# Attention and two feed-forward layers in one program: the second batch's values by probabilities in plain float32, and a new table of ranks

## The chip, the core and the metric

The kernel runs on one core of one Trainium2 chip. Five engines work side by side, each through its own list of instructions, strictly in order: TensorE (PE in the rows; its weight loads are PEld), VectorE (DVE), ScalarE (ACT), GpSimd (POOL) and SyncE (SP), which issues nearly all DMAs. They wait for each other by semaphores. The metric is the device time of one execution in microseconds (us). Three runs of the kernel before gave 1352.32, 1354.08 and 1358.2 us, a median of 1354.08.

## The reference

```python
# attention: batch 4, heads 8, seq 1152, head_dim 64
q_pool = q.reshape(B, H, S // 2, 2, D).mean(axis=3)          # 576 queries a head
scores = scale * np.matmul(q_pool, k.transpose(0, 1, 3, 2))
scores = scores - np.max(scores, axis=-1, keepdims=True)
attn = np.exp(scores)
attn = attn / (np.sum(attn, axis=-1, keepdims=True) + 1e-09)
x = np.matmul(attn, v)                                       # to 2304 tokens x 512
# first layer, d_ff 2048
r = np.maximum(x @ w_in, 0.0)
x = (s * (r * r) + b) @ w_out
# second layer, d_ff 1536
gate = 1.0 / (1.0 + np.exp(-(x @ w_gate)))
out = (gate * (x @ w_val)) @ w_out2
```

The weights come as 64-bit floats and are decoded on the chip.

## The kernel before

Nearly every product is done in three matmuls of the reduced type float32r: an operand is split into a high part (a rounding copy) and a low part (the remainder, a subtraction), and high by high, high by low and low by high add up in one bank of PSUM. The splits are work of ACT, POOL and DVE; the matmuls are work of PE.

Attention goes by batches and, in each, by 4 pairs of heads. The first batch is computed with queries as rows (`pair_rows`). The other three go by half heads (288 queries of one head; 16 to a batch) in `half_head_sums`. For each half head `scores` computes nine chunks of 128 keys by 288 queries (line 1350), copies them to three tiles `st` of 864 columns (ACT, line 909), takes a running maximum (DVE, line 915), turns that on PE (line 1363), reduces it (DVE, line 1367), spreads it over rows on PE (line 1324), subtracts it (DVE, line 915) and takes the exponential (ACT, line 1376). Then come the values by the probabilities. `split_p` makes a high copy (line 902 on ACT or 904 on POOL) and a low remainder (line 912, POOL or DVE) of each `st` tile in `pp` tiles. In batches 2 and 3 (`TWICE`) two matmuls a chunk follow, with the sums of the probabilities taken apart. In batch 1, the second one, three follow: line 1410 has [high values, ones] by the high probabilities, line 1411 the low values by the same, line 1416 [high values, ones] by the low probabilities; the block of ones gives the sums. The stationary tile `vt` (two of them, one to a head of a pair) holds 64 columns of low values, 64 of high values and 64 ones for each of nine chunks. `pair_prep` loads the values to `vn` and splits them into `vt`.

When a batch's attention is done, its tokens go through both layers (`feed`), 512 tokens for each of the first three feeds and 768 for the last. The first feed also decodes all weights: a DMA brings each block to `raw`, POOL, ACT and DVE turn it into float32 and split it, and a second DMA writes it to DRAM, from which the later feeds fetch it. So the attention of batch 1 runs beside the feed of batch 0, that of batch 2 beside the feed of batch 1, and so on.

What stands where in each engine's list is decided while the program is built. Each piece of work is handed to `Plan.add` with the engines that may do it and a key: the place `plan.here` on a scale (set by `ATTENTION` and `FEED`), plus a rank, plus an offset from the table `MOVED` under the work's name, or under the name with the batch's number behind it. `Plan.order` goes through a modelled time, and each free engine takes, of the work that is ready and for which buffers are free (`ROOM`: 6 `st`, 6 `pp`, 2 `vt`), the one with the lowest key. Work that may go to either of two engines goes to the one that is free.

Of the kernel before, what the change touches and what calls it, by code (L numbers as in the profile page):

```python
# [28 lines left out]
    yy=3, h=6, fo=6,  # L29
# [3 lines left out]
TWICE = (2, 3)  # L33
BANKS = {"wd", "pr", "ps", "pm", "acc", "ff", "p2", "sw"}
# [3 lines left out]
ATTENTION = (0.0, 154.358, 482.727, 814.266, 1198.726)  # L38
FEED = ((155.318, 486.674), (486.244, 871.22), (847.424, 1217.864), (1188.829, 2055.108))
# [3 lines left out]
    "q load": -46.791,  # L43
    "q load 0": 44.454,
    "q load 1": 86.533,
    "q load 2": 91.042,
    "k load": 232.645,
    "k load 0": -178.11,
    "k load 1": 67.466,
    "k load 2": -156.159,  # L50
    "v load": 220.491,
    "v load 0": 331.827,
    "v load 1": 667.448,
    "v load 2": 367.841,
    "v hi": 1.473,
    "v hi 1": -105.009,
    "v hi 2": 255.85,
    "v hi 3": -133.093,
    "v lo": -208.396,
    "v lo 0": -30.837,  # L60
    "v lo 1": -341.63,
    "v lo 3": -230.048,
    "q add": 25.255,
    "q add 0": -41.984,
    "q add 1": 44.956,
    "q add 2": 255.451,
    "q twice": 586.792,
    "q twice 0": 599.338,
    "q twice 2": 363.453,
    "q twice 3": 493.346,  # L70
    "pr qT": 40.098,
    "pr qT 0": -34.388,
    "pr qT 2": -687.648,
    "pr qT 3": -170.944,
    "pr q hi False": 8.875,
    "pr q hi False 1": -50.718,
    "pr q hi False 2": 14.122,
    "pr q hi False 3": 37.589,
    "pr q lo False": -456.003,
    "pr q lo False 1": -96.245,  # L80
    "pr q lo False 2": 251.737,
    "pr q lo False 3": -36.054,
    "pr q hi True": -95.229,
    "pr q hi True 0": 5.606,
    "pr q hi True 1": 326.988,
    "pr q hi True 2": 34.598,
    "pr q lo True": -20.002,
    "pr q lo True 2": -129.941,
    "pr q lo True 3": -59.474,
    "pr kT": 16.556,  # L90
    "pr kT 0": -242.646,
    "pr kT 1": 25.409,
    "pr kT 2": -9.23,
    "pr k hi": -33.36,
    "pr k hi 0": 4.807,
    "pr k hi 1": 196.142,
    "pr k hi 2": -33.136,
    "pr k lo": -142.294,
    "pr k lo 1": -27.449,
    "pr k lo 2": -205.53,  # L100
    "pr k lo 3": 55.312,
    "s b load": 512.259,
    "s b load 1": 1037.217,
    "s b load 2": 943.244,
    "s b load 3": 566.882,
    "r qk 1": -23.623,
    "r qk 1 1": -150.831,
    "r qk 1 2": 82.967,
    "r qk 1 3": -101.691,
    "r max": 331.04,  # L110
    "r max 0": -35.554,
    "r max 1": 131.697,
    "r max 3": 148.081,
    "r - max": -445.953,
    "r - max 0": -517.456,
    "r - max 2": -507.089,
    "r - max 3": -676.096,
    "r exp": 0.445,
    "r exp 1": -55.826,
    "r exp 2": -2.402,  # L120
    "r exp 3": 100.054,
    "r pT": -210.967,
    "r pT 0": -42.303,
    "r pT 1": -113.749,
    "r pT 2": -249.703,
    "r p 1": -48.074,
    "r p 2": -452.662,
    "r p 3": -28.185,
    "r p hi": -16.997,
    "r p hi 0": 14.026,  # L130
    "r p hi 1": -147.871,
    "r p hi 2": 43.781,
    "r p lo": -504.147,
    "r p lo 0": -251.61,
    "r p lo 1": -297.75,
    "r p lo 2": -406.012,
    "r pv": -175.215,
    "r pv 0": -123.32,
    "r pv 1": -108.239,
    "r pv 2": -13.038,  # L140
    "r pT hi 1": 273.656,
    "r pT hi 2": 38.298,
    "r pT hi 3": -483.679,
    "r pT lo": -1383.98,
# [1720 lines left out]
```

## Time and profile before

| | us |
|---|---|
| median of three runs | 1354.08 |
| the profiled execution, whole | 1354.87 |
| its span (first to last instruction) | 1353.0 |
| its mean granted TensorE clock | 0.998 |

A row "a:b" of the table by stretches gives, after the length, how long each engine was busy and its instructions. The span falls roughly into the first batch's attention alone (to 155 us), then the attention of batch 1 beside the first feed (155 to 487), that of batch 2 beside the second feed (487 to 820), that of batch 3 beside the third (820 to 1050), and the last feed. A matmul's busy time overlaps with that of the next, so the distance from start to start tells what one costs in a stream.

### The profile page before, as it was taken

Reading aid. Unit: us, or ns where it says so; the run is one execution under the profiler, and the core shown is the slowest. Engines: PE = TensorE matmul, PEld = TensorE weight load, DVE = VectorE, ACT = ScalarE, POOL = GpSimd, SP = SyncE. Lnnn points to the kernel's source line nnn. Section 1 sums busy time; section 2 is a strip of 40 time slices with the busy share of each in tenths; the row PEclk is TensorE's granted clock in tenths of the full one; section 3 lists DMA queues with packets and bytes.
Section 4 is the critical chain, followed back from the end, with each engine's and each line's share of the span. In section 5 each row is a group of like instructions: output and inputs, shape, how many; then the busy total and the mean of one; then the engine's idle time right before and its main releaser. Section 6 shows DMA issues by size and latency. Waiting matters only on the chain.

```text
span 1353.0 us, 22000 instructions
## 1 busy us (share of the span) xinstructions
PE 1308.0 (97%) x7596; PEld 1167.9 (86%) x7596; DVE 1146.4 (85%) x1857; ACT 925.7 (68%) x1957; POOL 944.1 (70%) x772
## 2 busy tenths in 40 slices
PE   7998999998989999999999999999999999999998
PEld 6887879898877888888888888888888899999997
DVE  6899998999979998999988987998988746678775
ACT  6898889888868777787677758676765354443321
POOL 3578768898978877687757768776766456546562
PEclk9999999999999999999999999999999999999999
DMA  3146325868666682535444444435333434345332
GB/s 97 53 116 215 98 77 183 276 198 281 232 230 229 234 268 102 173 139 173 139 157 154 151 163 160 157 107 205 125 134 124 152 131 154 129 152 185 126 125 47
DMA packets 98279, 214.88 MB, mean 159 GB/s; under 512 B 45148, under 2 KB 67448, under 8 KB 82040
## 3 DMA queue, kind: packets, MB, share of 16 engines
q1 hardware_dynamic: 97000, 213.18, 47.4%
q8 instruction: 60, 0.98, 0.3%
q14 instruction: 51, 0.42, 0.1%
q10 hardware_dynamic: 1168, 0.29, 0.1%
HBM read 173.02 MB, written 40.43 MB: 158 GB/s over the span
## 4 chain that ended last, share of the span: by engine, by line
PE 68%; DVE 9%; ACT 8%; POOL 5%; DMA 5%; issue 5%; SPq 0%; DVEq 0%; POOLq 0%; ACTq 0%
PE banks L985 11%; PE banks L987 11%; PE banks L986 10%; PE banks L1350 5%; PE banks L1698 3%; PE banks L1700 3%; PE banks L1699 3%; PE banks L1122 3%; PE banks L1124 3%; PE banks L1123 3%; PE banks L1416 3%; PE banks L1408 2%; DVE st L915 2%; DMA raw<-in_moe_w_val_dram 2%; PE banks L1506 2%
## 5 line engine op out<-in xcount | busy, mean ns | idle before, releaser
L912 POOL TENSOR_TENSOR pp<-st,pp 128x864 fp32r<-128x864 f32 x94 | 211.3, 2253 | 24.1 <-ACT pp L902 11.9
L915 DVE TENSOR_TENSOR st<-banks,st 128x288 f32<-128x288 f32 x384 | 171.9, 448 | 25.9 <-ACT st L909 10.6
L985 PE MATMUL banks<-xx,w 128*128 128x512 f32 x480 | 193.5, 403 | 0.0
L986 PE MATMUL banks<-xx,w 128*128 128x512 f32 x480 | 188.3, 392 | 0.4 <-POOL xx L912 0.3
L987 PE MATMUL banks<-xx,w 128*128 128x512 f32 x480 | 188.1, 392 | 0.0
L909 ACT COPY st<-banks 128x288 f32<-128x288 f32 x432 | 152.0, 407 | 34.7 <-PE banks L1350 27.2
L1350 PE MATMUL banks<-qT,kT 128*128 128x288 f32 x864 | 159.0, 301 | 5.7 <-ACT st L909 4.1
L915 DVE TENSOR_TENSOR st<-st,banks 128x864 f32<-128x864 f32 x144 | 148.2, 1041 | 3.3 <-PE banks L1324 3.0
L1376 ACT ACTIVATE st<-st 128x864 f32<-128x864 f32 x144 | 133.3, 936 | 24.6 <-DVE st L915 23.6
L1350 PEld LDWEIGHTS banks<-qT,kT 128*128 128x128 f32 x864 | 132.3, 188 | 18.0 <-ACT st L909 4.7
L902 ACT CAST pp<-st 128x864 fp32r<-128x864 f32 x120 | 109.4, 920 | 2.5 <-DVE u L912 1.7
L987 PEld LDWEIGHTS banks<-xx,w 128*128 128x128 f32 x480 | 90.1, 188 | 20.0
L986 PEld LDWEIGHTS banks<-xx,w 128*128 128x128 f32 x480 | 90.4, 188 | 12.6 <-POOL xx L912 1.3
L985 PEld LDWEIGHTS banks<-xx,w 128*128 128x128 f32 x480 | 90.4, 188 | 12.6 <-DVE raw L948 0.4
L986 PE MATMUL banks<-g,w 128*128 128x256 f32 (+1 forms) x256 | 86.6, 338 | 0.6 <-POOL g L912 0.6
L985 PE MATMUL banks<-g,w 128*128 128x512 f32 (+2 forms) x256 | 86.8, 339 | 0.0
L987 PE MATMUL banks<-g,w 128*128 128x512 f32 (+2 forms) x256 | 86.4, 338 | 0.0
L1416 PE MATMUL banks<-pp,vt 128*128 128x288 f32 x432 | 82.1, 299 | 2.5 <-DVE pp L912 1.7
L912 DVE TENSOR_TENSOR pp<-st,pp 128x864 fp32r<-128x864 f32 x50 | 78.1, 1562 | 6.2 <-ACT pp L902 3.7
L912 POOL TENSOR_TENSOR w<-raw,w 128x512 fp32r<-128x512 f32 x58 | 79.4, 1377 | 4.2 <-ACT w L902 3.6
L912 POOL TENSOR_TENSOR pp<-st,st 128x864 f32<-128x864 f32 x21 | 43.3, 2064 | 46.3 <-ACT st L1376 46.3
L1416 PEld LDWEIGHTS banks<-pp,vt 128*128 128x128 f32 x432 | 66.8, 190 | 5.6 <-DVE pp L912 2.4
(248 smaller groups left out, 4004.7 us busy)
## 6 DMA issues: line engine op xcount, KB each, us to landing
w<-d_2g_2v SPq DMA_DIRECT2D x26, 1024.0 KB, 4.9
w<-d_1u_1u SPq DMA_DIRECT2D x24, 1024.0 KB, 4.9
w<-d_1d_1d SPq DMA_DIRECT2D x24, 1024.0 KB, 5.0
w<-d_2d_2d SPq DMA_DIRECT2D x18, 1024.0 KB, 4.8
raw<-in_moe_w_out_dram SPq DMA_DIRECT2D x28, 512.0 KB, 4.3
d_2g_2v<-w SPq DMA_DIRECT2D x12, 1024.0 KB, 7.9
w<-d_2g_2v SPq DMA_DIRECT2D x20, 512.0 KB, 5.3
qn<-in_q_dram SPq DMA_DIRECT2D x16, 576.0 KB, 4.7
```

The costliest lines, as they stand in the source:

```text
L902: nc.scalar.copy(out=out(), in_=in_())
L909: act(name, n, lambda: nc.scalar.copy(out=out(), in_=in_()), r, w, rank, sbuf=False)
L912: shared(name, n, lambda e: ENGINE[e].tensor_tensor(out=out(), in0=in0(), in1=in1(), op=op), r, w, rank, 2.25)
L915: dve(name, n, lambda: nc.vector.tensor_tensor(out=out(), in0=in0(), in1=in1(), op=op), r, w, rank)
L985: nc.tensor.matmul(ps(), lhsT=whi(), rhs=xhi(), start=first, stop=False)
L986: nc.tensor.matmul((ps_lo or ps)(), lhsT=whi(), rhs=xlo(), start=False, stop=False)
L987: nc.tensor.matmul(ps(), lhsT=wlo(), rhs=xhi(), start=False, stop=last)
L1122: nc.tensor.matmul(ps.t[:, :n], lhsT=wt(0, a), rhs=xt(0, a), start=a == 0, stop=False)
L1123: nc.tensor.matmul(ps.t[:, :n], lhsT=wt(0, a), rhs=xt(1, a), start=False, stop=False)
L1350: nc.tensor.matmul(ps.t[:, :HQ], lhsT=kT.t[:, c], rhs=qq[:, w, hf * HQ:(hf + 1) * HQ], start=(w == 0), stop=(w == 1))
L1376: act("exp", 3 * HQ, lambda s=s: nc.scalar.activation(out=s.t[:, :3], in_=s.t[:, :3], func=AF.Exp), [], parts, AT)
L1416: nc.tensor.matmul(acc.t[:, :HQ], lhsT=vt.t[:, 3 * i + c, cols], rhs=lo.t[:, c], start=False, stop=(i == c == 2))
```

## The change

For the heads in `WHOLE`, all eight of batch 1, the values are no longer split: the DMA writes them into the middle third of a `vt` tile of plain float32. The probabilities aren't split either: one plain float32 matmul a chunk takes [values, ones] as the stationary operand and the `st` tile itself as the moving one. `values_slot` gives a `vt` tile of the kind that is wanted; where the kind changes, the block of ones is written anew (four times in the program).

The keys are changed as well: `ATTENTION` and `FEED` have other numbers, and a name now carries the pair of heads (" @0" to " @3") in attention and the quarter of the feed (" :0" to " :3") in a feed, so that `MOVED`, wholly replaced, can give each pair and quarter offsets of its own. So the order on all engines is another one, throughout the program.

```diff
 TWICE = (2, 3)
+WHOLE = [(1, h) for h in range(8)]
...
-ATTENTION = (0.0, 154.358, 482.727, 814.266, 1198.726)
+ATTENTION = (0.0, 153.708, 478.342, 810.481, 1176.021)
...
-    "p hi 1": 23.93,
+    "pv hi @2": 16.166,
...
     def add(self, name, engine, ns, issue, reads=(), writes=(), rank=0, holds=(), port=False):
+        name += self.part
...
+    def values_slot(kind, may):
+        new = []
+        def make(k):
+            if kinds[k] != kind:
+                assert may
+                uid[0] += 1
+                vts[k] = pools["hd"].tile([P, NK, 3 * D], kind, tag=f"vt{k}", bufs=1, name=f"vt{k}_{uid[0]}")
+                kinds[k] = kind
+                new.append(k)
+            return vts[k]
+        t = plan.slot("vt", make)
+        def fill(e):
+            to, of = t.t[:, :, 2 * D:], ones[:, :, None].to_broadcast([P, NK, D])
+            if new and e == "ACT":
+                nc.scalar.copy(out=to, in_=of)
+            elif new:
+                nc.gpsimd.tensor_scalar(out=to, in0=of, scalar1=1.0, scalar2=0.0, op0=ALU.mult, op1=ALU.add)
+        if may:
+            shared("v ones", NK * D, fill, [], [(t, 2)], AT, 0.95, act=0.833)
+        return t
...
+            if whole:
+                dma("v load", P * NK * D * 4, lambda t=t, src=src: nc.sync.dma_start(out=t.t[:, :, D:2 * D], in_=src),
+                    [], [(t, 0), (t, 1)], AT)
+                vt.append(t)
+                continue
...
+            if whole:
+                def issue_whole(s=s, i=i):
+                    for c in range(3):
+                        nc.tensor.matmul(acc.t[:, :HQ], lhsT=vt.t[:, 3 * i + c, D:], rhs=s.t[:, c],
+                                         start=(i == c == 0), stop=(i == c == 2))
+                pe("pv whole", 3 * mm(4 * HQ), issue_whole, [*((s, c) for c in range(3)), (vt, 0), (vt, 2)], [acc], SK)
+                continue
...
+            plan.part = f" :{int(4 * done[0] / total)}"
...
+            plan.part = f" @{hp}"
```

TensorE, the first probabilities of batch 1 by the values, in the kernel before: the three kinds of matmul on a third of a half head.

```order
L1410 MATMUL banks<-pp_2443,vt_111 128x288
L1411 MATMUL banks<-pp_2443,vt_111 64x288
L1410 MATMUL banks<-pp_2443,vt_111 128x288
L1411 MATMUL banks<-pp_2443,vt_111 64x288
L1410 MATMUL banks<-pp_2443,vt_111 128x288
L1411 MATMUL banks<-pp_2443,vt_111 64x288
L1416 MATMUL banks<-pp_2451,vt_111 128x288 x3
```

The same place of the changed program (its line 2559 is the new matmul, 2503 the scores, 2106 to 2108 the first layer, 2516 and 2477 the two steps of the maximum on PE).

```order
L2559 MATMUL banks<-st_2304,vt_1408_2108 128x288 x3
L2106 MATMUL banks<-xx_825,w_998 128x512
L2107 MATMUL banks<-xx_825,w_998 128x512
L2108 MATMUL banks<-xx_825,w_998 128x512
L2503 MATMUL banks<-qT_2142,kT_2211 128x288 x2
L2559 MATMUL banks<-st_2320,vt_1408_2108 128x288 x3
```

Nine float32r matmuls to a third have become three plain ones, which read `st` instead of `pp`.

TensorE, the maximum of batch 1's first half head, before: from the turn of the running maximum (line 1363) to its spreading over rows (line 1324).

```order
L1350 MATMUL banks<-qT_2135,kT_2155 128x288 x6
L1613 MATMUL banks<-ident,r_272_2189 128x128
L1363 MATMUL banks<-ident,st_2238 96x128 x3
L1610 MATMUL banks<-ident,pp_2387 128x128 x4
L1350 MATMUL banks<-qT_2135,kT_2155 128x288 x2
L1324 MATMUL banks<-ident,mc_2417 128x96 x3
```

And in the changed program, from line 2516 to line 2477:

```order
L2503 MATMUL banks<-qT_2143,kT_2212 128x288 x4
L2516 MATMUL banks<-ident,st_2304 96x128 x3
L2503 MATMUL banks<-qT_2143,kT_2212 128x288 x2
L2106 MATMUL banks<-xx_825,w_998 128x512
L2107 MATMUL banks<-xx_825,w_998 128x512
L2108 MATMUL banks<-xx_825,w_998 128x512
L2503 MATMUL banks<-qT_2143,kT_2212 128x288 x2
L2477 MATMUL banks<-ident,mc_2414 128x96 x3
```

Between the two steps PE had four turns and two matmuls of 288 columns; now it has four of 288 and three of 512.

SyncE, the second pair of heads of batch 1, before (`vn` takes the values, `raw` the weights to be decoded):

```order
L1253 DMA kn_3017<-in_k_dram 128x9x64 x2
L932 DMA raw_3059<-in_moe_w_in_dram 128x4x256
L1457 DMA r_d_150<-rs_2910 64x9
L934 DMA raw_3088<-in_moe_w_out_dram 128x1024
L974 DMA d_1d_1d_122<-w_2799 128x2048
L1461 DMA s_2613<-r_d_150 64x288 x2
L974 DMA d_1u_1u_123<-w_2998 128x2048
L1259 DMA vn_3189<-in_v_dram 128x576
L934 DMA raw_3203<-in_moe_w_out_dram 128x1024
```

And in the changed program:

```order
L2395 DMA qn_2857<-in_q_dram 128x1152
L2053 DMA raw_2875<-in_moe_w_in_dram 128x4x256
L2408 DMA vt_1408_2108<-in_v_dram 128x9x64
L2053 DMA raw_2899<-in_moe_w_in_dram 128x4x256
L2400 DMA kn_2917<-in_k_dram 128x9x64 x2
L2095 DMA d_1d_1d_121<-w_2811 128x2048
```

The load of values goes straight to `vt`, with weights and keys queued behind it.

## Rows read from the trace of the kernel before

**Rows 1.** The page's first part: busy time, share, instructions.

```profile
PE 1308.0 (97%) x7596; PEld 1167.9 (86%) x7596; DVE 1146.4 (85%) x1857; ACT 925.7 (68%) x1957; POOL 944.1 (70%) x772
```

**Rows 2.** Stretches: length; busy us (count) of PE, PEld, DVE, ACT, POOL; clock, DMA.

```profile
0.00:155.00 155.00, 134.95 (x914) 120.29 (x915) 134.89 (x302) 131.62 (x384) 102.27 (x132) 1.00 0.41 121
155.00:487.00 332.00, 316.92 (x1975) 281.01 (x1974) 304.16 (x558) 274.29 (x559) 279.01 (x252) 0.99 0.65 212
487.00:820.00 333.00, 329.52 (x1850) 285.35 (x1849) 301.81 (x444) 246.98 (x493) 239.55 (x170) 1.00 0.47 157
```

**Rows 3.** PE in order of time: start us, us, line, operands, count.

```profile
317.18 0.28 PE L985 MATMUL banks<-g,w 128*128 128x256 f32 x1
317.30 0.28 PE L986 MATMUL banks<-g,w 128*128 128x256 f32 x1
...
379.10 0.40 PE L1699 MATMUL banks<-w,g 128*128 128x512 f32 x1
379.33 0.40 PE L1700 MATMUL banks<-w,g 128*128 128x512 f32 x1
...
382.02 0.29 PE L1410 MATMUL banks<-pp,vt 128*128 128x288 f32 x1
...
382.82 0.56 PE L1416 MATMUL banks<-pp,vt 128*128 128x288 f32 x3
```

**Rows 4.** Matmuls of 155 to 487 us by form: count, busy us, mean ns, idle before.

```profile
L985 PE MATMUL banks<-xx,w 128*128 128x512 f32 x160 | 65.2, 407 | 0.0
L1350 PE MATMUL banks<-qT,kT 128*128 128x288 f32 x296 | 57.4, 304 | 5.4 <-ACT st L909 4.1 <-DVE st L915 0.9 <-ACT w L902 0.2
L1410 PE MATMUL banks<-pp,vt 128*128 128x288 f32 x132 | 37.5, 304 | 0.9 <-ACT pp L902 0.9
L986 PE MATMUL banks<-g,w 128*128 128x256 f32 x128 | 36.2, 283 | 0.6 <-POOL g L912 0.6
L1698 PE MATMUL banks<-w,g 128*128 128x512 f32 x32 | 12.8, 400 | 0.0
```

**Rows 5.** PE in order of time, around the one plain float32 matmul, line 1553.

```profile
75.14 0.33 PE L1553 MATMUL banks<-ident,st 128*128 128x64 f32 x2
75.31 0.39 PE L1551 MATMUL banks<-ident,st 128*128 128x128 f32 x2
75.53 0.33 PE L1553 MATMUL banks<-ident,st 128*128 128x64 f32 x2
```

**Rows 6.** A wait of PE in 155 to 487 us: total, times, longest.

```profile
PE banks L1324 <- DVE mc L1367: 4.2, 5, 1.2
```

**Rows 7.** All engines in order of time, around PE's longest wait there.

```profile
385.77 0.65 POOL L937 TENSOR_SCALAR raw<-raw 128x512 f32<-128x512 f32 x1 [4.36 <-DMA raw<-in_moe_w_gate_dram]
386.45 0.73 ACT L940 ACTIVATE raw<-raw 128x512 f32<-128x512 f32 x1 [3.86 <-POOL raw L937]
...
387.51 0.53 PE L1350 MATMUL banks<-qT,kT 128*128 128x288 f32 x2 [4.13 <-ACT st L909]
```

**Rows 8.** Line 1553 alone: records, ns min/median/max, first and last start.

```profile
L1553 PE MATMUL banks<-ident,st x144: 221/248/275, 27.1 to 173.0; 128*128 128x64 f32 x144
```

**Rows 9.** The tile pp in 155 to 487 us, columns as in rows 8.

```profile
L912 POOL TENSOR_TENSOR pp<-st,pp x35: 2045/2074/2865, 189.0 to 479.3; 128x864 fp32r<-128x864 f32 x35
L902 ACT CAST pp<-st x34: 894/922/963, 189.3 to 478.1; 128x864 fp32r<-128x864 f32 x34
...
L904 POOL TENSOR_SCALAR pp<-st x11: 912/920/1714, 188.0 to 452.4; 128x864 fp32r<-128x864 f32 x11
L912 DVE TENSOR_TENSOR pp<-st,pp x10: 1045/1224/2135, 190.4 to 476.0; 128x864 fp32r<-128x864 f32 x10
```

**Rows 10.** DMA issues (count, KB, median us to landing), and a wait of SyncE.

```profile
vn<-in_v_dram SPq DMA_DIRECT2D x32, 288.0 KB, 4.3
kn<-in_k_dram SPq DMA_DIRECT2D x31, 288.0 KB, 4.6
...
SPq L1259 <- POOL vt L912: 70.3, 16, 14.6
```

More of the change, by code (lines that the diff above doesn't have):

```diff
@@ L612, in __init__ @@
         self.room, self.loose, self.banks, self.moved = dict(room), loose, banks, moved
-        self.stage, self.here = 0, 0.0
+        self.stage, self.here, self.part = 0, 0.0, ""
         self.ops, self.last, self.readers, self.queue = [], {}, {}, {}
@@ L1257, in pair_prep @@
             src = v[b, h0 + j].rearrange("(p c) d -> p c d", c=NK)
+            whole = (b, h0 + j) in WHOLE
+            t = values_slot(F32 if whole else F32R, any(divmod(8 * b + h0 + j - i, 8) in WHOLE for i in range(5)))
+            if whole:
[3 more added lines that the diff above has]
+                continue
             vn = slot("ld", "vn", [P, NK, D])
             dma("v load", P * NK * D * 4, lambda vn=vn, src=src: nc.sync.dma_start(out=vn.t, in_=src), [], [vn], AT)
-            t = plan.slot("vt", lambda k: vts[k])
             copy_sb("v hi", NK * D, lambda t=t: t.t[:, :, D:2 * D], lambda vn=vn: vn.t, [vn], [(t, 0)], AT)
@@ L1386, in split_p, with half_head_sums @@
         return hi, lo
-    def half_head_sums(hf, j, qT, kT, vt, x, sums, rows, twice):
+    def half_head_sums(hf, j, qT, kT, vt, x, sums, rows, twice, whole):
         st = scores(hf, qT, kT)
@@ L1416, in issue_lo @@
                     nc.tensor.matmul(acc.t[:, :HQ], lhsT=vt.t[:, 3 * i + c, cols], rhs=lo.t[:, c], start=False, stop=(i == c == 2))
-            pe("pv hi", (3 if twice else 6) * mm(HQ), issue_hi, [hi, (vt, 0), (vt, 1)], [acc], SK)
-            pe("pv lo", 3 * mm(HQ), issue_lo, [lo, (vt, 0), (vt, 1)], [acc], SK)
+            pe("pv hi", (3 if twice else 6) * mm(HQ), issue_hi, [hi, (vt, 0), (vt, 1), (vt, 2)], [acc], SK)
+            pe("pv lo", 3 * mm(HQ), issue_lo, [lo, (vt, 0), (vt, 1), (vt, 2)], [acc], SK)
         if twice:
@@ L1429, in issue_sums @@
                     nc.tensor.matmul(total.t[:D, :HQ], lhsT=vt.t[:, 0, 2 * D:], rhs=u.t[:, w], start=(w == 0), stop=(w == 1))
-            pe("all sums", 2 * mm(HQ), issue_sums, [(u, 0), (u, 1), (vt, 0)], [total], SK)
+            pe("all sums", 2 * mm(HQ), issue_sums, [(u, 0), (u, 1), (vt, 0), (vt, 2)], [total], SK)
             r0 = 0
@@ L1473, in pair_half @@
             at(hf / 2 + j / 4)
-            half_head_sums(hf, j, qT[j], kT[j], vt[j], (xt, xk), sums, D if last else 1, b in TWICE)
+            half_head_sums(hf, j, qT[j], kT[j], vt[j], (xt, xk), sums, D if last else 1, b in TWICE, (b, 2 * hp + j) in WHOLE)
         both = [(sums, 0), (sums, 1)]
@@ L1789 @@
         open_pool(attention, name)
-    vts = [pools["hd"].tile([P, NK, 3 * D], F32R, name=f"vt{k}") for k in range(2)]
+    vts = [pools["hd"].tile([P, NK, 3 * D], F32R, tag=f"vt{k}", bufs=1, name=f"vt{k}") for k in range(2)]
     for t in vts:
         nc.vector.tensor_copy(out=t[:, :, 2 * D:], in_=ones[:, :, None].to_broadcast([P, NK, D]))
+    kinds = [F32R, F32R]
     pairs = [(b, hp) for b in range(B) for hp in range(NP)]
```

1511 lines of the change are left out of this document (980 added, 531 removed), and 670 rows, old and new, of the table MOVED.

## The prediction, made before the changed kernel ran

> **What bounds the kernel now.** I read the busy shares first: PE is busy for 97% of the span, the next engine for 85% [rows 1]. So the question is where PE loses time, and the table by stretches answers it [rows 2]: PE idles for 155.00 - 134.95 = 20 us in the first batch's attention, for 332.00 - 316.92 = 15.1 us beside batch 1, and for only 333.00 - 329.52 = 3.5 us beside batch 2. The two later stretches are alike in PE's work but not in that of the others: ACT has 274 us beside batch 1 and 247 beside batch 2, POOL 279 and 240, DVE 304 and 302, the share of the DMA engines is 0.65 and 0.47.
>
> Busy time hides part of the loss, since a matmul's record overlaps the next. From start to start a matmul of 512 columns costs 379.33 - 379.10 = 0.23 us, one of 256 0.12, and one of 288 0.133: from 382.02 to 382.82 there are six, on lines 1410 and 1411 in turn [rows 3]. Beside batch 1 there are 576 of 512 columns (lines 985, 986 and 987 have 160 each, 1698, 1699 and 1700 have 32 each), 692 of 288 (296 of the scores, 132 on each of lines 1410, 1411 and 1416) and 384 of 256 or 258 (128 on each of lines 985, 986 and 987) [rows 4]; the other 323 of the 1,975 [rows 2] are nearly all transposes, at (75.53 - 75.31) / 2 = 0.11 [rows 5]. That is 132 + 92 + 46 + 36 = 306 us of 332, so some 26 us are lost there, where the idle time says 15. The waits that have a name are on the maximum from DVE, 4.2 us in five pieces [rows 6], and one of 4.1 us on a copy by ACT. That one comes from the stream of weights: POOL had waited 4.36 us for a load of gate weights, ACT's next work for POOL, and PE for ACT [rows 7].
>
> **The change part by part.**
>
> *PE, the price.* Batch 1 has 16 half heads of nine chunks, 144 chunks. Before, each takes three float32r matmuls, 3 x 0.133 = 0.40 us. The trace has no plain float32 matmul of 288 columns, but one of 64, line 1553. One instruction of it stands as two records with a weight load each; the first is followed by the second some 0.055 us later (0.33 for both [rows 5], less the longest record, 0.275 [rows 8]), and from the first start to the next line's it is 75.31 - 75.14 = 0.17 us. 0.055 us for 64 columns is 0.86 ns a column, about two clocks of the 2.4 GHz level (granted 1.00 there [rows 2]); 288 columns at that rate are 0.247 us. Low end: both records run like a float32r one, 0.266 us, or 19 us less than before. High end: the pair scales whole, 0.17 x 4.5 = 0.765 us, 53 us more. I take the value by the first record, two passes of 0.247, 0.494 us: (0.494 - 0.40) x 144 = **+13.5 us**, all on the engine that bounds. The 0.11 us that follow the second record of line 1553 are a weight load that 64 columns don't cover; 288 columns at 0.24 do.
> The Trainium skill, "FP8 and Floating Point Precision", section "TensorE Precision Notes", says that true FP32 takes 4 passes through the array. Reckoned so, 4 x 288 columns at 2.4 GHz are 0.48 us, and the term would be +11.5 instead of +13.5; the trace shows two records, not four, each at about twice the time a column, which is the same amount of work.
>
> *ACT, POOL and DVE, what goes.* Each of the 48 `st` tiles of batch 1 loses a high copy (0.92 us on ACT or POOL) and a low remainder (2.07 on POOL, 1.22 on DVE). In the stretch beside batch 1 these are 34 x 0.92 = 31 us of ACT, 35 x 2.07 + 11 x 0.92 = 83 us of POOL and 10 x 1.22 = 12 us of DVE [rows 9], and the eight splits of the values go too. So there ACT comes to about 240 of 332 us and POOL to about 195, both below what they have beside batch 2; DVE to 290, below its 302 there. None of that is on PE's path by itself: it is worth what PE waited for. What comes in is four writes of ones; nothing of POOL's or ACT's size.
>
> *What PE gets back.* With ACT, POOL and DVE no busier than beside batch 2, PE should lose there in the proportion of batch 2's stretch: 3.5 / 15.1 of 26 us is 6 us. But weights may come late as they did [rows 7], since no weight load goes away, so I leave one such 4.1 us in: about 10 us. That gives back **16 us** of 26; the ends are 0 and 26. The step also drops two links of the chain from exponential to matmul, high copy and remainder, 0.92 + 2.07 us of waiting that PE no longer needs to cover. In return the `st` tile stays held until PE has read it, where the remainder freed it before; six of them are two half heads, so the scores of the next half head but one now wait on PE's own list, not on POOL. That is hidden as long as the first layer's matmuls stand between.
>
> *The loads of the values.* Before, SyncE's load went to a spare `vn` and waited there for POOL, 70.3 us in 16 pieces [rows 10], with POOL's and ACT's splits behind. Now it waits for PE's last read of that `vt`, and weights, keys and queries queue up behind it on SyncE. Each `vt` of a pair has the other head's half between its last use and its next, some 332 / 16 = 20 us against 4.6 us of landing, so I cost it at nothing; uncovered it is a rival below. The load now lands in runs of 64 floats, 256 bytes, as the keys' load already does: 4.6 us against 4.3 [rows 10].
> The Trainium skill, "DMA: Bandwidth & Descriptors", section "Specifications", wants at least 512 bytes for line rate, which speaks against such a load. If that doubled it, each would land some 4 us later; the rows show 0.3, and with 20 us of lead neither changes the sum.
>
> *The new order.* With offsets for each pair and quarter, everything moves. The order shows at batch 1's first maximum that PE has 4 x 0.133 + 3 x 0.23 = 1.2 us of work between turn and spread, where it had 4 x 0.11 + 2 x 0.133 = 0.7: half a us more cover for a step that PE waited for in that stretch [rows 6]. No row prices the rest. PE idles 45 us in all (1353.0 less 1308.0 [rows 1]), 20 of them in the first stretch and 10 after 487 us [rows 2]; those 30 are the low end, -30; the high end is one more stretch that loses like batch 1's, +15. I take **-7**, a quarter of the low end: work on ACT and DVE in the first stretch (132 and 135 of 155 us [rows 2]) is unchanged in kind, so most of its 20 us should stay.
>
> Sum: the profiled execution is 1354.87 us, 0.8 above the median of the runs. 1354.87 + 13.5 - 16 - 7 = 1345.4; I say **1345 us**, 0.7% less.
>
> **Rivals.**
>
> *Only a swap.* PE pays 13.5 us and gets about as much back, because its losses beside batch 1 come less from ACT and POOL than from weights that arrive late and from DVE, which loses only 12 of 304 us. For it: of PE's named waits only 0.9 us is on a copy of the probabilities [rows 4], the longest is the weights' [rows 7], and DVE stays the busiest beside PE. Against it: the loss from start to start is 26 us where the idle time is 15, many small waits rather than a few. Then 1354.87 + 13.5 - 14 = 1354 us.
>
> *The values' load holds up SyncE (slower).* Six of the eight loads stand among the weights to be decoded. Where one stands ahead of its release, the weights behind it come late and PE stops, as before 387.51, for 4.1 us [rows 7]. For it: SyncE has waited up to 14.6 us at such a load [rows 10]. Against it: the 20 us of lead, and that the wait is now for PE alone and no longer for POOL behind it. Price: six times 4.1 is 25 us, and 1354.87 + 13.5 - 16 - 7 + 25 = 1370 us. It decides from three such stops on, for with them the gain is gone.
>
> *The plain matmul costs more than its columns (slower).* If the weight load between the two records isn't covered, the price is 53 us, not 13.5, and the time 1354.87 + 53 - 16 - 7 = 1385 us. Against it: a fixed gap of 0.11 us fits line 1553 better than a factor.
>
> *The new order gives much.* If the first stretch's idle time goes by half and batch 1's loss to 6 us: 1354.87 + 13.5 - 20 - 15 = 1333 us. For it: the table's offsets now differ by pair; against it: that stretch's ACT and DVE are busy for 85 and 87%.
>
> **How the numbers follow.** A measurement of this kernel can tell about 0.5%, 7 us, from no change. Forecast (1337 to 1348): 0.40; the new order gives much: 0.16; only a swap (1348 to 1361): 0.27; the load holds up SyncE: 0.10; the matmul costs more, or the order turns out worse in another stretch: 0.07. 0.5% below the median is 1347.3 and 0.5% above it 1360.9, so the first two make up "faster" but for 0.02, the swap "same", and the rest "slower": faster 0.54, same 0.29, slower 0.17. The range that leaves out a tenth at each end is 1327 to 1364; that of the likeliest alone is the 1337 to 1348 above.
>
> **What would show it right or wrong.** In the profile of the changed kernel line 2559 should stand as 288 records with starts 0.24 to 0.25 us apart; 0.13 or 0.38 would throw the first term out. In the stretch beside batch 1 ACT should be near 240, POOL near 195 and DVE near 290 us, and PE's idle time below 6 us. If POOL and ACT fall like that but PE's waits on DVE and on copies stay, the swap is right. If SyncE waits long at line 2408 and POOL's line for the weights waits for DMA more than before, the third rival is. If batch 1 comes out as said but the total doesn't, look at the first stretch's 20 us.

## The result: slower by half a per cent

| kernel | median, us | runs | ratio to the kernel before, 95% interval |
|---|---|---|---|
| before | 1352.67 | 7 | |
| changed | 1359.98 (1359.04 to 1363.35) | 7 | 1.0052 [1.0036, 1.0068] |

The forecast was 1345 with 0.17 on slower; the time lies inside the wide range, but the likeliest case was wrong, and so was the sign. The changed kernel's profiled execution took 1359.90 us.

The changed kernel's page, its first part, and then its table by stretches, columns as in [rows 1, 2]:

```profile
PE 1317.9 (97%) x7452; PEld 1164.2 (86%) x7452; DVE 1135.7 (84%) x1855; ACT 891.6 (66%) x1905; POOL 827.6 (61%) x718
```

```profile
0.00:155.00 155.00, 135.10 (x905) 120.72 (x906) 134.69 (x303) 130.46 (x379) 100.96 (x128) 0.99 0.40 121
155.00:487.00 332.00, 321.88 (x1833) 274.10 (x1831) 289.39 (x546) 236.60 (x502) 183.62 (x210) 1.00 0.64 208
487.00:820.00 333.00, 330.39 (x1823) 284.73 (x1822) 298.62 (x439) 241.90 (x487) 238.80 (x168) 1.00 0.47 161
820.00:1050.00 230.00, 227.05 (x1254) 195.86 (x1253) 200.40 (x286) 163.13 (x321) 151.64 (x100) 1.00 0.39 134
1050.00:1358.00 308.00, 303.46 (x1645) 288.80 (x1643) 212.60 (x285) 119.50 (x220) 152.53 (x114) 1.00 0.40 138
```

Beside batch 1, DVE, ACT and POOL came out at 289, 237 and 184 us, where 290, 240 and 195 were forecast: the engines were relieved as reckoned. PE's idle time there fell only from 15.1 to 332.00 - 321.88 = 10.1 us, not below 6, and the first stretch still idles 20 us. The engines got their relief and PE did not get its time.

The plain float32 matmul did what the forecast said. PE in order of time, from 386 us on (start, length, line, operands, records):

```profile
386.06 3.08 PE L2559 MATMUL banks<-st,vt 128*128 128x288 f32 x12
388.97 0.27 PE L2433 MATMUL banks<-ident,kn 128*128 128x128 f32 x1
389.08 1.62 PE L2559 MATMUL banks<-st,vt 128*128 128x288 f32 x6
390.54 0.49 PE L2516 MATMUL banks<-ident,st 128*96 128x128 f32 x3
```

Twelve records in 388.97 - 386.06 = 2.91 us and six in 1.46 are 0.243 us each: 0.485 for the two records of a matmul, against 0.494 forecast.

What POOL waited for beside batch 1, the changed kernel (engine, tile and line, releaser; total us, times, longest):

```profile
POOL raw L2058 <- DMA raw<-in_moe_w_out_dram: 33.6, 15, 5.5
POOL g L2306 <- PE banks L2108: 12.8, 5, 9.2
POOL w L2025 <- PE banks L2108: 12.4, 4, 5.8
POOL w L2025 <- PE banks L2861: 11.5, 3, 9.0
POOL w L2033 <- ACT w L2023: 9.0, 8, 3.1
POOL raw L2058 <- DMA raw<-in_moe_w_gate_dram: 8.9, 6, 2.8
POOL raw L2058 <- DMA raw<-in_moe_w_val_dram: 6.9, 4, 4.5
```

POOL (line 2058 is line 937 of before) now waits 49 us for packed weights in these three rows. In the kernel before the same line waited much less, 16 us with two shorter waits that are left out here:

```profile
POOL raw L937 <- DMA raw<-in_moe_w_gate_dram: 9.1, 6, 4.4
...
POOL raw L937 <- DMA raw<-in_moe_w_val_dram: 3.8, 3, 2.8
```

By the forecast's own list of signs that speaks for the values' load holding up SyncE. But SyncE's waits at that load (line 2408; SPq is SyncE's queue of DMA issues) are one long one and a few short ones:

```profile
SPq L2408 <- PE banks L2734: 15.5, 1, 15.5
...
SPq L2408 <- PE banks L2503: 6.5, 1, 6.5
SPq L2408 <- PE banks L2559: 4.3, 2, 2.2
```

With two shorter ones these are 28.2 us. In the kernel before SyncE stood at the values' load (line 1259) in the same stretch for almost as long, 27.2 us:

```profile
SPq L1259 <- POOL vt L912: 15.4, 3, 14.6
SPq L1259 <- DVE vt L912: 11.8, 1, 11.8
```

The two longest waits of the changed kernel ended at its first two loads of values, at 162.2 and 180.6 us, before the first load of packed weights beside batch 1 (193.8; 195.1 in the kernel before). At the six loads that stand among the weights SyncE waited 6.2 us in all. So it is not SyncE standing at these loads that lengthens POOL's waits.

**How losses are counted below.** For one profiled execution of each kernel I gave every instruction of PE the distance from start to start that its shape has when nothing is late (0.227 us for 512 columns, 0.173 for 384, 0.132 for 288, 0.114 for 256, 0.242 for a record of line 2559). Their sum is PE's work, what is left of the time is lost; some 11 us of each span, ahead of PE's first matmul and behind its last, are in neither. The borders are the last product of the first batch's attention and the last scores of batches 1, 2 and 3, so that they move with the kernel:

| us | work | lost, first attention | batch 1 | batch 2 | batch 3 | last feed | lost in all |
|---|---|---|---|---|---|---|---|
| before | 1259 | 36.2 | 28.2 | 9.5 | 7.0 | 2.0 | 82.9 |
| changed | 1272 | 37.9 | 18.5 | 8.6 | 8.0 | 2.3 | 75.3 |

PE's work grew by 12.7 us and its losses fell by 7.6; the rest is +5.1, as the profiled executions differ (1359.90 - 1354.87 = 5.0). The forecast had the losses fall by 16 + 7 = 23.

### The profile page after: what moved, and what is told of

It reads as the page before. It is cut to its first block, busy times and chain, and to the rows that moved or that the text cites. A ratio compares the mean times of both kernels' runs of the same rounds, so it can differ in the third digit from the quotient of the medians.

```text
span 1358.1 us, 21565 instructions
## 1 busy us (share of the span) xinstructions
PE 1317.9 (97%) x7452; PEld 1164.2 (86%) x7452; DVE 1135.7 (84%) x1855; ACT 891.6 (66%) x1905; POOL 827.6 (61%) x718
## 4 chain that ended last, share of the span: by engine, by line
PE 74%; DVE 9%; DMA 6%; issue 4%; ACT 4%; POOL 2%; SPq 0%; DVEq 0%; POOLq 0%; ACTq 0%
PE banks L2106 11%; PE banks L2107 11%; PE banks L2108 11%; PE banks L2503 6%; PE banks L2859 4%; PE banks L2861 4%; PE banks L2860 4%; PE banks L2243 3%; PE banks L2245 3%; PE banks L2244 3%; PE banks L2577 2%; PE banks L2569 2%; DVE st L2036 2%; PE banks L2559 2%; PE banks L2667 2%
## 5 line engine op out<-in xcount | busy, mean ns | idle before, releaser
L2033 POOL TENSOR_TENSOR pp<-st,pp 128x864 fp32r<-128x864 f32 x53 | 123.2, 2331 | 11.7 <-ACT pp L2023 5.7
L2023 ACT CAST pp<-st 128x864 fp32r<-128x864 f32 x89 | 81.1, 919 | 3.9 <-POOL u L2033 3.1
L2033 POOL TENSOR_TENSOR w<-raw,w 128x512 fp32r<-128x512 f32 x54 | 73.3, 1363 | 13.7 <-ACT w L2023 12.7
L2559 PE MATMUL banks<-st,vt 128*128 128x288 f32 x288 | 77.3, 409 | 3.8 <-ACT st L2529 2.3
L2058 POOL TENSOR_SCALAR raw<-raw 128x512 f32<-128x512 f32 x63 | 42.1, 668 | 61.2 <-DMA raw<-in_moe_w_out_dram 33.6
L2033 POOL TENSOR_TENSOR pp<-st,st 128x864 f32<-128x864 f32 x23 | 49.1, 2136 | 46.0 <-ACT st L2529 45.0
L2033 DVE TENSOR_TENSOR pp<-st,pp 128x864 fp32r<-128x864 f32 x43 | 68.5, 1594 | 3.4 <-POOL u L2033 1.8
```

The source lines that it names most:

```text
L2023: nc.scalar.copy(out=out(), in_=in_())
L2033: shared(name, n, lambda e: ENGINE[e].tensor_tensor(out=out(), in0=in0(), in1=in1(), op=op), r, w, rank, 2.25)
L2559: nc.tensor.matmul(acc.t[:, :HQ], lhsT=vt.t[:, 3 * i + c, D:], rhs=s.t[:, c], start=(i == c == 0), stop=(i == c == 2))
```

## The experiments

All times are medians; the kernel before, run beside each set, took 1352.8, 1352.5, 1352.75, 1351.0 and 1353.0 us.

| run | us | ratio [95%] |
|---|---|---|
| new_ranks_f32r: old arithmetic, new order | 1365.5 | 1.0093 [1.0073, 1.0114] |
| old_ranks_f32: new arithmetic, old order | 1383.4 | 1.0227 [1.0206, 1.0248] |
| third_split: old order, relief without PE's price | 1346.7 | 0.9958 [0.9945, 0.9971] |
| narrow228: new order, relief without PE's price | 1357.1 | 1.0031 [1.0017, 1.0044] |
| raw4_after, raw4_aligned: changed, four buffers | 1355.9, 1351.3 | 1.0020 [1.0009, 1.0031], 0.9988 [0.9975, 1.0000] |
| raw4_before: before, four buffers | 1346.0 | 0.9949 [0.9929, 0.9969] |
| raw4_narrow: narrow228, four buffers | 1350.8 | 0.9988 [0.9978, 0.9997] |
| raw4_narrow_aligned, the same again as four_new_order | 1346.6, 1347.8 | 0.9973 [0.9964, 0.9982], 0.9962 [0.9946, 0.9977] |
| raw4_third, the same again as four_old_order | 1340.0, 1341.8 | 0.9907 [0.9886, 0.9928], 0.9918 [0.9900, 0.9937] |
| short_max: changed, DVE relieved | 1361.9 | 1.0063 [1.0044, 1.0082] |
| half_keep: changed, fewer writes of weights | 1358.6 | 1.0038 [1.0024, 1.0053] |
| jitter_before_1, jitter_after_1: ranks moved by up to 3 us | 1398.6, 1391.6 | 1.0334 [1.0311, 1.0356], 1.0304 [1.0286, 1.0321] |
| jitter_before_half, jitter_after_half: by up to 0.5 us | 1372.0, 1375.1 | 1.0156 [1.0142, 1.0170], 1.0181 [1.0166, 1.0197] |

### The two parts of the change, one without the other

```diff
-WHOLE = [(1, h) for h in range(8)]
+WHOLE = []          # new_ranks_f32r: the changed kernel, batch 1 split as before
```

> The new ranks with the old arithmetic: no head is computed whole, so batch 1 keeps its split probabilities and three float32r matmuls a chunk. Theory 1 (the swap: the arithmetic costs PE 12.7 us and gives back less, the new ranks give nothing): about 1350 to 1356 us, the time of the kernel before. Theory 2 (the new ranks are the loss, the arithmetic a gain): 1362 us or more. Theory 3 (the new ranks gain some 7 us as predicted, the arithmetic loses more than it gains): 1346 us or less.

For old_ranks_f32 the changed kernel got `ATTENTION`, `FEED` and `MOVED` of the kernel before, and names without the pair or quarter.

> The new arithmetic with the old ranks and keys (names without pair and quarter). Theory 1 (swap): 1353 to 1360 us, near the changed kernel's 1360. Theory 2 (ranks are the loss): 1345 us or less. Theory 3: 1362 us or more, since ranks found for the other arithmetic also order this one.

Each part alone is slower: 12.7 and 30.7 us. The first time fits theory 2, the second theory 3, so none of the three holds. Together the parts are 7.3 slower, so the two are not a sum: the new order costs 12.7 us under the old arithmetic and gains 23.4 (1383.4 to 1360.0) under the new one. Under the old arithmetic it loses even beside batch 2, whose work the change leaves alone. In new_ranks_f32r PE idles 7.2 us there, in the changed kernel 2.6, in the one before 3.5:

```profile
487.00:820.00 333.00, 325.75 (x1799) 280.18 (x1798) 299.07 (x431) 238.47 (x480) 245.82 (x170) 0.99 0.46 157
```

Each table belongs to its arithmetic, and a change of arithmetic under the old table says little about the arithmetic.

### Relief and price apart

narrow228 keeps the changed kernel's order and takes PE's price away:

```diff
-nc.tensor.matmul(acc.t[:, :HQ], lhsT=vt.t[:, 3 * i + c, D:], rhs=s.t[:, c],
+n = HQ if i == c == 0 else 228
+nc.tensor.matmul(acc.t[:, :n], lhsT=vt.t[:, 3 * i + c, D:], rhs=s.t[:, c, :n],
...
```

> The changed kernel in its own order on every engine, but eight of the nine plain float32 matmuls of a half head take 228 of their 288 columns (the other 60 queries miss those keys), so that PE's work in batch 1 is what three float32r matmuls cost: 16 x 8 x 2 x 60 x 0.84 ns = 12.9 us less. If PE's added work is wholly exposed (theory 1): 1360 - 12.9 = 1347 us, and that is what the relief of the other engines is worth. If it lies beside waits that stay (the chain over DVE and the weights bounds batch 1's stretch): 1354 us or more.

third_split keeps the order and the matmuls of the kernel before and splits only a third of each tile in batch 1 (PE reads that third three times):

```diff
+m = 1 if plan.stage == 1 else 3
-copy_sb("p hi", 3 * HQ, lambda: hi.t, lambda: s.t[:, :3], parts, [hi], SK)
+copy_sb("p hi", 3 * HQ, lambda: hi.t[:, :m], lambda: s.t[:, :m], parts, [hi], SK)
...
```

> The kernel before in its own order, but in batch 1 the split of the probabilities covers one third of each tile and the matmuls read that third three times (the other two thirds of the probabilities are left out): ACT loses some 22 us, POOL some 55, DVE some 8, PE's work is the same. If PE's losses beside batch 1 come from ACT, POOL and DVE being busy (my prediction's step): about 10 us less, 1343 us. If they come from the maximum's chain and the weights' loads (the swap): 1349 us or more.

Of narrow228's two cases the second came, waits that stay. third_split's 1346.7 lies between its two.

| us | work | lost, first attention | batch 1 | batch 2 | batch 3 | last feed | lost in all |
|---|---|---|---|---|---|---|---|
| third_split | 1259 | 36.7 | 21.0 | 8.4 | 5.8 | 2.0 | 73.9 |
| narrow228 | 1260 | 38.7 | 27.6 | 9.2 | 7.9 | 2.3 | 85.7 |

Three steps lead from before to changed. Relief in the old order: 1352.7 to 1346.7, -6.0 for two thirds of it. From third_split to narrow228, at equal work of PE: 1346.7 to 1357.1, +10.4, although narrow228 has all of the relief. PE's price in the new order: 1357.1 to 1360.0, +2.9; the intervals of these two ratios overlap, but it is far from 12.7. The +10.4 holds more than the order: in narrow228 the values' loads also go straight to `vt`, and `st` is held until PE has read it. No run parts these from the order. It is also one way from before to changed; through old_ranks_f32 the steps are +30.7 and -23.4. Of 12.9 us of work taken off PE some 10 came back as losses, 9.1 of them in batch 1 (18.5 to 27.6). From border to border batch 1 takes 259.8 + 27.6 = 287.4 us without the price and 270.3 + 18.5 = 288.8 with it: something other than PE set its pace.

### What sets the pace beside batch 1: four theories

A block of packed weights goes through one of three buffers `raw`: a load by SyncE, then work of POOL, ACT and DVE. By pairing each load with the last instruction on its buffer, I found a buffer held for 14.8 us on average in the kernel before; 56 blocks of that on three buffers make 276 us, and these loads were issued over 274 us. In the changed kernel it is 15.0 us, 55 blocks and 275.6 of 273 us: hardly a buffer is ever free, with the engines relieved or not. That was theory W, that the stream of weights through three buffers sets the pace. The others were DVE's chain (D), contention of the DMA engines, and the order itself (O).

In raw4_after and raw4_narrow a fourth buffer lies in the space of `u`, which only the attention of batches 2 and 3 needs (not the second layer, as the expectation has it), and of `qm`, which only that of the first batch needs:

```diff
+def make(k):
+    p, g = ("sm", "u0") if tag == "raw" and k == 3 else (pool, f"{tag}{k}")
+    return view(pools[p].tile(shape, dtype, tag=g, bufs=1, name=name))
...
+    if s.tag == "raw":
+        first, last = of[s]
+        e = min(x for x in ends if x[0] < first
+                and (x[1] < 3 or start < first and last < end))
+        ends[ends.index(e)] = (last, e[1])
+        s.k = e[1]
...
```

> The changed kernel with its own order; a fourth buffer for the packed weights, carved out of space that only the second layer needs, is used from the second pair of batch 1's scores until that space is wanted, where there were three. Nothing is left out. Three theories of why batch 1's stretch gave so little back. W, the stream of weights paces it: a buffer is held some 15 us, three of them serve one block per 5 us, and all three are held the whole time; with a fourth the loads come a third earlier, the waits of POOL for loads (33.6 us on the output weights beside batch 1) fall by more than half, and the time falls by 8 us or more, to 1352 or less. D, DVE's chain of maxima and reductions paces it: no change, 1360 (1356 to 1363). O, the order alone is at fault (each step stands where its rank puts it, and nothing is late): no change either, 1360.

> As the kernel with the narrowed plain matmuls (eight of nine take 228 of 288 columns, so that PE's price is taken away; the rest of the columns' values is left out), with the fourth buffer for packed weights. That kernel took 1357.1 with three. By W the 12.7 us of PE that were taken away only now come off: 1344 or less. By D and O no change: 1357 (1354 to 1360).

```diff
+m = 96 if b == 1 and c > 1 else HQ      # short_max
-tt_dve("s max", HQ, mxt, lambda ps=ps: ps.t[:, :HQ], ...
+tt_dve("s max", HQ, lambda m=m: mxt()[:, :m], lambda ps=ps, m=m: ps.t[:, :m], ...
```

> The changed kernel with its own order; in batch 1 the running maximum of the scores looks beyond chunk 1 at 96 of 288 columns only (the other columns' maximum is taken over two chunks, a part of the computation left out), which takes some 28 us off DVE in that stretch, and shortens each half head's chain. By D PE's waits on the maxima go and the time falls by 6 us or more, to 1354 or less. By W and by O: 1360 less at most 2.

```diff
-w_d[key] = dram.tile([P, 2, 2, 512], F32, ...)      # half_keep
+w_d[key] = dram.tile([P, 1, 2, 512], F32, ...)
-dma("w keep", ..., in_=s.t.bitcast(F32)), parts, [key], rank)
+dma("w keep", ..., in_=s.t[:, :1].bitcast(F32)), parts, [key], rank)
...
```

> The changed kernel with its own order; only one half of each decoded weight block is written to memory, and that half is fetched for both halves, so the products with the other half are left out. It takes half the writes of decoded weights off the DMA engines. By a theory of contention (the DMA engines are 0.64 busy beside batch 1, so packed weights land late behind the writes): POOL's waits for loads fall and the time falls by 5 us or more, to 1355 or less. By W without contention, D and O: no change, 1360 (1357 to 1363).

DVE's running maxima are out as the pace: DVE's busy time beside batch 1 fell by 19 us (some 28 were meant), PE's didn't rise, and the time was 1361.9, no shorter than 1360.0. short_max, the same stretch:

```profile
155.00:487.00 332.00, 320.81 (x1836) 274.17 (x1834) 270.16 (x544) 236.17 (x504) 183.63 (x210) 1.00 0.64 206
```

Contention is out as a main cause: with the share of the DMA engines down from 0.64 to 0.55 the time went down by 1.4 us, less than the intervals can tell, where 5 were expected. half_keep:

```profile
155.00:487.00 332.00, 322.65 (x1850) 276.61 (x1849) 292.11 (x549) 238.06 (x508) 183.90 (x210) 1.00 0.55 163
```

raw4_after gained 4.1 us where W wanted 8 and the others none, and raw4_narrow came to 1350.8 where W wanted 1344 and the others 1354 or more. raw4_after's losses in batch 1 fell from 18.5 to 10.6, but the last feed, which has no packed weights, lost 5.2 instead of 2.3. I had cut two other tiles to make room, and with that PE's matmuls there had become slower one by one (last section). Without the cuts:

```diff
-s_sb = const.tile([P, 1], F32, name="s_sb")
+s_sb = const.tile([P, 32], F32, name="s_sb")[:, :1]
-return slot("fg", "g", [P, 2 * TB + 8], F32R)
+return slot("fg", "g", [P, 2 * TB + 32], F32R)
```

> The changed kernel with four buffers for packed weights, as the run of that kind before, but without the two tiles that were cut to 1 and to 1032 columns there, so that every other buffer begins where it does in the changed kernel. Nothing is left out. In that run PE's matmuls of 384 and of 512 columns went from 173 to 175 and from 227 to 232 ns in the last stretch, 2.9 us in all. If the place of the buffers did that, it goes: 1353 (1351 to 1354.5). If not: 1356 as there.

> The kernel before with its own order and arithmetic, and the fourth buffer for packed weights as in the changed kernel with four. Nothing is left out. W, the stream of weights paces batch 1's stretch in both kernels: the losses of PE there (28.2 us by starts) fall by some 8 us as they did in the changed kernel (18.5 to 10.6), and the time to 1346 or less. O, only the new order draws on weights in a way that three buffers can't serve: 1352 (1350 to 1355).

> The kernel before with its own order, only a third of each tile of batch 1's probabilities split (a part of the computation left out, which takes two thirds of the work off ACT, POOL and DVE), now with the fourth buffer for packed weights. With three it took 1346.7. If the buffers are what keeps the relief of the engines from PE: PE's losses beside batch 1 fall from 21.0 to 12 us or less, and the time to 1339 or less. If they are not: 1346.7 (1344 to 1349).

The fourth buffer is worth 8.7 us in the changed kernel (1360.0 to 1351.3), 6.8 in the kernel before (1352.75 to 1346.0) and 6.7 under third_split (1346.7 to 1340.0). The stretch beside batch 1, raw4_before:

```profile
155.00:487.00 332.00, 322.34 (x2023) 287.18 (x2022) 312.66 (x573) 281.68 (x573) 288.73 (x260) 1.00 0.67 220
```

and raw4_aligned:

```profile
155.00:487.00 332.00, 326.64 (x1873) 280.82 (x1873) 297.31 (x560) 242.53 (x515) 186.63 (x213) 1.00 0.66 215
```

PE idles 9.7 us in the first (15.1 with three buffers) and 5.4 in the second (10.1), while no engine got less to do. So W holds, for the kernel before as much as for the changed one: there the time was to fall to 1346 or less. raw4_third, at 1340.0, with 15.1 us lost beside batch 1 (four_old_order, the same kernel), came to neither of its two cases. As an explanation of the change it holds less: what leaving out two thirds of the splits gives is about the same with three buffers (6.0) and with four (6.0, or 4.2 by the second pair of runs below). The two gains add up; the buffers did not keep the relief from PE. What kept it is not shown.

POOL's waits for loads are a poor measure of it. In raw4_aligned the one on output weights is

```profile
POOL raw L2075 <- DMA raw<-in_moe_w_out_dram: 13.6, 9, 4.2
```

20 us less than with three buffers, for a gain of 8.7; in the kernel before all of POOL's waits for packed weights were some 16 us, and the gain was 6.8. The length of these waits is not a price.

### Is the new order worse because of the three buffers?

> The changed kernel with the fourth buffer (every other buffer at its old place) and the narrowed plain matmuls: eight of nine take 228 of 288 columns, the rest of the columns' values is left out, and PE's extra work is gone. The same with three buffers took 1357.1; the old order with equal PE work and four buffers took 1340.0. If the new order is worse only because three buffers serve it badly: 1341 or less, 10 us under the 1351.3 of the changed kernel with four. If it loses elsewhere too: 1347 to 1350.

> The old order with four buffers and a third of the splits of batch 1 (as before, a part of the computation left out), now on one chip with the narrowed kernel of the new order with four buffers. 1340 as it was, or 1338.5 where the kernel before takes 1351.

> The new order with four buffers and narrowed plain matmuls (a part of the computation left out), PE's work equal to the other's. With three buffers the two orders lay 10.4 us apart. If the three buffers were most of that: within 4 us of the other run. If they were not: 6 to 10 us above it.

| us | work | lost, first attention | batch 1 | batch 2 | batch 3 | last feed | lost in all |
|---|---|---|---|---|---|---|---|
| raw4_before | 1259 | 36.0 | 19.4 | 9.5 | 7.0 | 2.0 | 73.9 |
| raw4_aligned | 1272 | 38.3 | 11.1 | 7.8 | 7.9 | 2.3 | 67.3 |
| four_old_order | 1259 | 37.5 | 15.1 | 8.1 | 7.0 | 2.0 | 69.7 |
| four_new_order | 1260 | 37.4 | 16.8 | 8.1 | 7.9 | 2.3 | 72.5 |

Side by side on one chip the two orders, at equal work of PE, are 1347.8 - 1341.8 = 6.0 us apart with four buffers, where it was 10.4 with three. So some 4 us of the 10.4 may come from the three buffers; from raw4_third and raw4_narrow_aligned, which are the same two kernels on other chips, the ratios lie 0.9973 - 0.9907 apart, 8.9 us, which would leave only 1.5. The rest does not come from the buffers: by the count of one execution of each only 2.8 us show, 1.7 in batch 1 and 0.9 in batch 3; where the others go I have not found. PE's price is worth 1351.3 - 1347.8 = 3.5 us with four buffers (4.7 by raw4_narrow_aligned), hardly more than the 2.9 with three, and not the 12.7 that W wanted.

### How closely a table fits its kernel

```diff
-key = self.here + rank + self.moved.get(self.named(name), 0.0)
+key = self.here + rank + self.moved.get(self.named(name), 0.0) + Random(f"1 {self.named(name)}").uniform(-3, 3)
```

> The kernel before, with each step's rank moved by a random amount of up to 3 us either way. Nothing is left out. If the table fits this kernel closely, so that any other order is worse, as the new table under the old arithmetic was by 12.7 us: 1358 or more. If the order matters little as long as each step stands roughly where it does: 1353 (1350 to 1356).

> The changed kernel with each step's rank moved by a random amount of up to 3 us either way. Nothing is left out. If its table fits it as closely as the old one fitted the old kernel (where the like cost 46 us): 1385 or more. If the new table is a loose fit, so that it has something to gain from another order: within 15 us of 1360, on either side.

> The kernel before with each step's rank moved by up to 0.5 us either way. Nothing is left out. A sixth of the amount that cost 46 us: 8 us if the cost goes with the amount, 1360; if each exchange of two steps counts whatever its size, 1365 or more; if small shifts don't matter, 1353 (1350 to 1356).

> The changed kernel with each step's rank moved by up to 0.5 us either way. Nothing is left out. As the one before: 1368 if the cost goes with the amount, 1373 or more if each exchange counts, 1360 (1357 to 1363) if small shifts don't matter; below 1357 the new table has room.

The random amount hangs on a step's name, so that all steps of one name move alike; the changed kernel has more names. Half a microsecond either way costs 21 us in the kernel before (1372.0 against 1351.0) and 15 in the changed one (1375.1 against 1360.0); three cost 46 and 32. Both tables sit in a narrow spot, and the cost doesn't go with the amount. The first attention stretch, which the change leaves alone in kind, pays a part of it: it lost 44.4 us in either kernel at half a microsecond, against 36.2 and 37.9. jitter_before_half there:

```profile
0.00:155.00 155.00, 130.97 (x864) 117.70 (x865) 128.57 (x290) 127.02 (x362) 97.88 (x124) 0.98 0.40 121
```

One seed was tried for each. A table that is off by half a microsecond costs more than this change does; that narrow228 is some 10 us behind third_split at equal work may need no mechanism of its own. That it is only a matter of fit is argued, not shown: no better table was tried for the new arithmetic.

## Why the prediction was wrong

Two terms of its sum failed, both on the side of the gain: what PE gets back beside batch 1 (-16, measured -9.7) and the new order (-7, measured +2.1 outside batch 1). Term by term:

- **"PE, the price: +13.5 us".** As an amount of work it held: 288 records 0.243 us apart, +12.7. "All on the engine that bounds" did not hold: taking it away gave 2.9 us with three buffers and 3.5 with four, in the new order. The busy share of 97% [rows 1] hid that PE was paced by others beside batch 1.
- **"ACT, POOL and DVE, what goes".** Held within 4 us for ACT and DVE and 11 for POOL.
- **"What PE gets back: 16 us".** Failed in size. The step was "PE should lose there in the proportion of batch 2's stretch". Beside batch 2 no packed weights are decoded; in the kernel before, the last loads of them stand at 475 us:

```profile
L934 SPq DMA_DIRECT2D raw<-in_moe_w_out_dram x28: 328/328/887, 104.3 to 474.6; - x28
```

  So the two stretches were not alike once ACT, POOL and DVE were, and the one 4.1 us wait that I "left in" for late weights [rows 7] was too little: a fourth buffer alone gave the kernel before 6.8 us, and 6.7 with two thirds of the splits gone, so this relief does not give them back. Measured: -6.0 for two thirds of the relief in the old order, and 28.2 to 18.5, -9.7 in place of -16, by the count in batch 1.
- **"The loads of the values ... at nothing".** No run measures this by itself, but the rows bear it out: SyncE stood at the values' loads beside batch 1 for 28.2 us, and for 27.2 in the kernel before, and the 15.5 us wait had no packed weights behind it. In raw4_aligned, which is 8.7 us faster, it stood there for 38.5. So the stops from which that rival decides did not come. The loads of the changed kernel (issues, KB each, median us to landing):

```profile
vn<-in_v_dram SPq DMA_DIRECT2D x24, 288.0 KB, 3.6
...
vt<-in_v_dram SPq DMA_DIRECT2D x8, 288.0 KB, 4.0
```

  The runs of 256 bytes landed in 4.0 us, below the 4.6 that the forecast allowed and below the 4.3 of `vn` in the kernel before [rows 10]; the 3.6 are of loads beside other batches. The Trainium skill, "DMA: Bandwidth & Descriptors", section "Specifications", asks for at least 512 bytes a transfer for line rate; no run here shows a loss by it.
- **"The new order: -7".** This is the larger miss. It took a quarter of the idle time outside batch 1 as gain, with no row that priced it. By the count, the stretches other than batch 1 lost 54.7 us before and 56.8 in the changed kernel: +2.1 in place of -7. The first of them, from which most of it was to come, lost 37.9 us instead of 36.2. Under the old arithmetic the new order cost 12.7 us. The cover for PE's wait on the maximum did come (4.2 us before, 1.4 in the changed kernel, below); what it was worth was not measured.

```profile
PE banks L2559 <- ACT st L2529: 2.3, 5, 0.7
PE banks L2559 <- DVE raw L2069: 1.5, 1, 1.5
PE banks L2477 <- DVE mc L2520: 1.4, 2, 0.9
```

- **The rivals.** "Only a swap" had part of the mechanism, losses that come from weights that arrive late, and came nearest, 6 us low. Its other half, DVE, fell with short_max, and it has no loss by the order, so that it came so near is in part luck. "The values' load holds up SyncE" is out by the rows above. "The plain matmul costs more" is out by the records; "the new order gives much" was the opposite of what came.

Put together by the count: +12.7 (price) - 9.7 (losses beside batch 1) + 2.1 (losses elsewhere) = +5.1, where the forecast had 13.5 - 16 - 7 = -9.5. Either miss alone, 6.3 or 9.1 us, would have left the changed kernel no slower than the one before; together they turned the sign. By the medians of the runs, along one of the ways between the two kernels: -6.0 (two thirds of the relief) + 10.4 (new order and all else at equal work) + 2.9 (price) = +7.3. How much of the losses is the order's and how much the new arithmetic's stays open.

A version that beats both comes out of it: raw4_before, the kernel before with the fourth buffer, 1346.0 us, ratio 0.9949 [0.9929, 0.9969].

## What to carry to other kernels

Before a stretch is forecast after another one that "is as busy", look what else only one of them has; here it was the decoding of weights, and the sign of it was that the buffers of its stream were nearly always held. A price on the busiest engine counts in full only where that engine sets the pace, and the waits of a relieved engine are no measure of what it is worth to end them. Where an order by a fitted table is replaced, put no gain on it without a row: half a microsecond of shift cost 15 to 21 us here, more than the whole change.

## What the runs showed of the hardware

A plain float32 matmul of 288 columns runs as two records, each 0.243 us apart at a granted clock of 1.00 (the 2.4 GHz level): about two clocks a column and record, 0.485 us for the whole, against 0.132 for one in float32r.

Where an operand begins can cost PE one or two per cent. In raw4_after two tiles had been cut to make room, and other buffers began elsewhere: by the layout of the two programs, the weights `w` begin 96 bytes and `yy` 480 bytes ahead of where they do in raw4_aligned. The same matmuls of the last feed, 384 columns on `yy`, in raw4_after, nine of them from first to last row:

```profile
1244.77 0.34 PE L2262 MATMUL banks<-yy,w 128*128 128x384 f32 x1
...
1246.35 0.34 PE L2262 MATMUL banks<-yy,w 128*128 128x384 f32 x1
```

and in raw4_aligned, which has the tiles at their old size:

```profile
1242.69 0.33 PE L2261 MATMUL banks<-yy,w 128*128 128x384 f32 x1
...
1244.25 0.33 PE L2261 MATMUL banks<-yy,w 128*128 128x384 f32 x1
```

1.58 / 9 = 0.1756 us against 1.56 / 9 = 0.1733. The medians there are 175 and 173 ns, and 232 and 227 for 512 columns of line 2876 (2859 in the changed kernel); the last feed lost 2.9 us by it, and raw4_aligned was 4.5 us faster in all. raw4_narrow and raw4_narrow_aligned differ by the same two tiles alone, and their medians are 175 and 173, 232 and 227 as well. The scores' matmuls of 288 columns stay at 133 ns in all four. Not every other start costs something: `w`, `yy` and `h` (line 2876 reads it) begin 2048 bytes earlier in raw4_aligned than in the changed kernel, since `qm` has left its place (its expectation has them where they were), and the medians are the same 173 and 227. Which of the two tiles did it, and which start is a good one, was not tried.
